# Moving one gate/up block between a down projection and its Wo part in a fused attention + GLU kernel

## The chip, the core and the metric

The program runs on one core of a Trainium2 chip. The metric is the device time of one execution in microseconds (us), lower is better. Engines are named as in the profile: PE (matrix engine, PEld its weight loads), DVE (vector), ACT (scalar, activations), POOL (GpSimd), SP (the queue that issues nearly all DMAs). All of them run their own instruction list strictly in the order in which the program was written; waiting is done with semaphores.

## The reference

One LayerNorm feeds two branches, and both are added to the input:

```
x  = A_x                              # 1 x 2048 x 640, bf16
xn = layernorm(x)                     # no weights, eps 1e-5
q, k, v = split(xn @ wqkv)            # 32 heads of 20
s  = q k^T * 20**-0.5, key j kept for query i if 0 <= i - j < 256
A  = (softmax(s) v) @ wo
B  = (sigmoid(xn @ w_gate) * (xn @ w_up)) @ w_down      # hidden width 1536
out = x + A + B
```

`B_x` is not used.

## The kernel before

**Tiling.** The 2048 rows are four chunks of 512. A chunk is four blocks of 128 rows (s = 0 to 3). Heads go in eight groups of four.

**Two streams of work.** The attention scores are the clock of the program. There are 76 scores steps, t = 0 to 75: chunk 0 has 0 to 15, chunk 1 has 16 to 35, chunk 2 has 36 to 55, chunk 3 has 56 to 75. A step is some 24 small matmuls (`ps`, L462), one big exponential on ACT (L467) and, for most steps, three masks on POOL (L470). The scores tile `ps` takes four PSUM banks and has one buffer, so the matmuls of step t+1 wait until the exponential of step t has read it. When all steps of two groups are through, `pv` (L487) multiplies with v (`acc`, L494), and DVE transposes the two sums (`t1`, L504).

Everything else is filler that PE does between two scores steps. It is written as generators that yield the PE time of each piece in ns: a projection `q` or `k` (5 matmuls, 1080), a `v` block (10 matmuls, 1360), gate `g` and up `u` of one of twelve gate/up blocks (1080 each; ACT makes the tanh `th`, DVE the product `h`; `th` has one buffer, L140), a quarter of a down projection `d` (6 matmuls, 816; four of them make the two column halves of one output block), and `W`, the ten matmuls with Wo that finish the output block (1360; then DVE adds x, L427, and SP stores, L436). The list of generators is at L642 to L662, and PE executes it in that order. At each step the loop at L678 gives out an allowance: the filler left up to the next output part (`out0`, `out1`, `out2`, or the end), divided by the steps left until it opens. Whole pieces are pulled until the allowance is used up (`credit`, L694); what is pulled too much is kept as debt. `out0` opens at step 17, `out1` at 36, `out2` at 56, each after the `pv` of the chunk's last two groups.

**Scaling the attention sums.** After `pv`, the division by the softmax sum (`scale_group`, L510: reciprocal, products into `on`, transposes into `oc`) isn't written at once. It is put into `fill.behind`, and each filler piece with a cost takes one entry off, after its own instructions (L542). The five tiles `oc` of a chunk are the weights of its `W` matmuls; the last one is complete only with the last group.

**LayerNorm.** Chunks 1 to 3 are normalised while the filler runs. `g_norms` (L333) has steps of no PE cost, called L (statistics on DVE), r (the inverse root on POOL), N (the normalised block on DVE) and T (`turn_block`, L275: a DMA transpose issued by SP into `xnT`). All four blocks of `xnT` must have landed before the first `q` of the chunk, since each matmul of a projection streams all 512 rows. `mix` (L564) puts one such step after every second piece of another generator. For chunk 2 (`norms2`) it starts in `gu1a` and goes on in `out0`.

**PSUM.** All other matmul results share a ring of four one-bank buffers (`ps_d`, L142): y0, y1 of an output block, pg, pu, pqk, pv, acc. A new tile takes the buffer of the fourth one before it and waits for its reader.

**The order that results** for the steps that the text speaks of. It is worked out from the costs and the allowance rule above; `S` is one scaled group, `P` the `pv` of two groups. A step's own scores come first, then the pieces:

```
 5: T N u S T T g S    13: v S v S          17: d S L r d S d
 6: u g u              14: v v              18: L r d W N d
 7: g u                15: g L u            19: d r N d d T N W
 8: q q P              16: g L r u P        20: d T N d d P
                                            21: T T d S W S d
36: d S d S T d d      56: d S d S d        22: d d d W
37: W T d d            57: d W              23: q q     (x of chunk 3 is loaded first)
```

In steps 12 to 14 this goes with `k k P`, `v v`, `v v`, where SP gets the loads of k and q of chunk 1 after the first and second `v`, and the load of Wo (four DMAs) at step 15. In step 62 there are two `d` alone.

Of the kernel before, what the change touches and what calls it, by code (L numbers as in the profile page):

```python
# [21 lines left out]
NG = H // HG  # L22
# [85 lines left out]
def kernel(  # L108
# [13 lines left out]
    out2 = out.flatten_outer_dims()  # L122
# [151 lines left out]
    def turn_block(c, s):  # L274
        nc.sync.dma_start(out=xnT[c][:, :, s * P:(s + 1) * P], in_=xns.pop((c, s)), transpose=True)  # L275
# [57 lines left out]
    def g_norms(c, turn):  # L333


        new_xnT(c)
        mv, rstd = {}, {}
        for k in range(SBC + 4):
            if k < SBC:
                mv[k] = ln_block(c, k)  # L340
            if 0 <= k - 1 < SBC:
                rstd[k - 1] = rstd_block(mv[k - 1])
            if k < SBC:
                yield 0
            if 0 <= k - 3 < SBC:
                norm_block(c, k - 3, mv[k - 3], rstd[k - 3])
                yield 0
            if turn and 0 <= k - 3 - 1 < SBC:
                turn_block(c, k - 3 - 1)

    def g_turns(c):
        for s in range(SBC):
            turn_block(c, s)
            yield 0

    def g_qk(c):
        for w in "qk":
            for m in range(DC):
                proj_block(w, c, m)
                if c == 0 and w == "q" and m == 1:  # L360
                    load_x(1)
                if w == "k" and m == 1:
                    spread("q", c, 0, GH if c else 2)
                yield 5 * MM
        if c == 0:
            spread("k", c, 0, 1)
            spread("k", c, 1, 3)
            spread("q", c, 2, 4)
            spread("k", c, 3, 4)
# [17 lines left out]
    def part(w, d, f):  # L387
        k, first = divmod(f * P, FS)
        return w[k][:, d, first:first + P]

    def g_gu(c, f0, f1):
        for f in range(f0, f1):
            pg = ps_d.tile([P, CW], FP32, name="pg", tag="d")
            for d in range(DC):
                nc.tensor.matmul(pg, lhsT=part(wg, d, f), rhs=xnT[c][:, d, :],  # L395
                                 start=(d == 0), stop=(d == DC - 1))
            th = tp.tile([P, CW], FP32, name="th")
            nc.scalar.activation(out=th, in_=pg, func=TANH, scale=0.5)  # L398
            yield 5 * MM
            pu = ps_d.tile([P, CW], FP32, name="pu", tag="d")  # L400
            for d in range(DC):
                nc.tensor.matmul(pu, lhsT=part(wu, d, f), rhs=xnT[c][:, d, :],  # L402
                                 start=(d == 0), stop=(d == DC - 1))
            h = hp.tile([P, CW], BF16, name="h")
            ht[c, f] = h
            nc.vector.scalar_tensor_tensor(out=h, in0=th, scalar=1.0, in1=pu, op0=ADD, op1=MULT)  # L406
            yield 5 * MM
# [6 lines left out]
    def down(c, s, y, cut):  # L414
        for f in range(FC):
            nc.tensor.matmul(y[:, 0:cut[1] - cut[0]], lhsT=ht[c, f][:, s * P:(s + 1) * P],  # L416
                             rhs=wd[:, f, cut[0]:cut[1]], start=(f == 0), stop=False)
            if f % 6 == 5:
                yield 6 * 136

    def add_wo(c, s, y, cut):
        for m in range(DC):
            nc.tensor.matmul(y[:, 0:cut[1] - cut[0]], lhsT=oc[c, m][:, s * P:(s + 1) * P],  # L423
                             rhs=wo[:, m, cut[0]:cut[1]], start=False, stop=(m == DC - 1))

    def add_x(c, s, y, cut, rows):
        nc.vector.scalar_tensor_tensor(  # L427
            out=rows[:, cut[0]:cut[1]], in0=y[:, 0:cut[1] - cut[0]], scalar=0.5,
            in1=xc[c][:, s, cut[0]:cut[1]], op0=MULT, op1=ADD)

    def new_rows():
        return lnp.tile([P, D], BF16, name="xn", bufs=5)

    def store(c, s, rows, cut=(0, D), queue=nc.sync):
        sb = c * SBC + s
        queue.dma_start(out=out2[sb * P:(sb + 1) * P, cut[0]:cut[1]], in_=rows[:, cut[0]:cut[1]])  # L436

    def outp(c, s, ys):
        rows = new_rows()
        for y, cut in zip(ys, HALVES):  # L440
            add_wo(c, s, y, cut)
        for y, cut in zip(ys, HALVES):
            add_x(c, s, y, cut, rows)
        store(c, s, rows)

    def g_out(c):
        for s in range(SBC):
            ys = [ps_d.tile([P, CW], FP32, name=f"y{i}", tag="d") for i in range(2)]
            for y, cut in zip(ys, HALVES):
                yield from down(c, s, y, cut)  # L450
            outp(c, s, ys)
            yield 10 * 136

# [33 lines left out]
    def pv(c, g, parts):  # L487
        acc = ps_d.tile([P, CW], FP32, name="acc", tag="d")
        flat = [(pt, *piece[1:]) for step, pt in parts for piece in step["pv"] if piece[0] == g]
        for k, (pt, r, q, n, col) in enumerate(flat):  # L490
            v = vt[c * SBC + r]
            for i in range(HG):
                h = g * HG + i
                nc.tensor.matmul(  # L494
                    acc[32 * i:32 * i + 32, q * U:(q + n) * U],
                    lhsT=v[:, h * VW:h * VW + 32], rhs=pt[:, i, col * U:(col + n) * U],
                    start=(k == 0), stop=(k == len(flat) - 1), skip_group_check=True)
        finish_group(c, g, acc)
# [3 lines left out]
    def finish_group(c, g, acc):  # L502
        t1 = np_.tile([P, 16, 32], FP32, name="t1")
        nc.vector.transpose(out=t1.rearrange("p b r -> p (b r)"), in_=acc)  # L504
        if c < NCH - 1 or g < NG - 2:
            fill.behind.append(lambda: scale_group(c, g, t1))
        else:
            scale_group(c, g, t1)
# [14 lines left out]
    class Fill:  # L523
        def __init__(self):
            self.parts = []
            self.behind = []
            self.done = set()
            self.shut = set()

# [8 lines left out]
        def one(self):  # L538
            label, gen, _ = self.parts[0]
            try:  # L540
                cost = next(gen)
                if cost and self.behind:  # L542
                    self.behind.pop(0)()
                self.parts[0][2] -= cost
                return cost
            except StopIteration:
                self.parts.pop(0)
                self.done.add(label)
                return 0
# [14 lines left out]
    def mix(a, b, first, every=1, rest=True):  # L564

        for k, cost in enumerate(a):
            yield cost
            if k >= first and (k - first) % every == 0:
                yield next(b, 0)
        if rest:  # L570
            yield from b
# [63 lines left out]
    fill = Fill()  # L635
    GU = 10 * MM
    OUT = 4 * 34 * 136
    def later(load, *args):
        load(*args)
        yield 0  # L640

    norms2 = g_norms(2, True)  # L642
# [5 lines left out]
    fill.add("qk1", g_qk(1), 50 * MM)  # L648
    fill.add("v1", g_v(1), 40 * 136)
    fill.add("wo", later(load_wo), 0)  # L650
    fill.add("gu1a", mix(g_gu(1, 0, 2), norms2, 0, 2, False), 2 * GU)
    fill.add("out0", mix(g_out(0), norms2, 0, 2), OUT)
    fill.add("x3", later(load_x, 3), 0)
    fill.add("qk2", g_qk(2), 50 * MM)
    fill.add("v2", g_v(2), 40 * 136)
    fill.add("gu1b", mix(g_gu(1, 2, 12), g_norms(3, False), 10), 10 * GU)
    fill.add("out1", mix(g_out(1), g_turns(3), 1, 3), OUT)
    fill.add("qk3", g_qk(3), 50 * MM)
    fill.add("v3", g_v(3), 40 * 136)
    fill.add("gu2", g_gu(2, 0, 12), 12 * GU)  # L660
    fill.add("out2", g_out(2), OUT)
    fill.add("gu3", g_gu(3, 0, 12), 12 * GU)  # L662

    todo = [(c, k, step) for c in range(NCH) for k, step in enumerate(steps_of(c))]
    ends = {}
# [13 lines left out]
    for t, (c, k, step) in enumerate(todo):  # L679
        if k == 0 and c > 0:  # L680
            fill.until(f"qk{c}")
        if k == 2 and c > 0:
            fill.until(f"v{c}")
        if t in due:
            fill.flush()
        for group in due.get(t, []):
            pv(*group, parts.pop(group))
            if group[1] == NG - 1:
                fill.shut.discard(f"out{group[0]}")
        made = (step, scores(c, step))  # L690
        for g in dict.fromkeys(piece[0] for piece in step["pv"]):
            parts.setdefault((c, g), []).append(made)
        last, label = next(x for x in cuts if t < x[0])
        credit += fill.left(label) / (last - t)  # L694
        credit = fill.pull(credit)
# [3 lines left out]
    c = NCH - 1  # L699
# [18 lines left out]
    s = SBC - 1  # L718
# [41 lines left out]
```

## Time and profile before

| what | value |
|---|---|
| runs | 317.76, 317.27, 316.70 us; median 317.27 us |
| the profiled execution's own time | 316.61 us |
| its span, first to last instruction | 314.9 us (1.7 us lie around it) |
| PE busy, as the profile counts | 305.2 us, 97% |
| DVE, ACT, POOL busy | 50%, 61%, 51% of the span |
| granted PE clock | 1.000 over the whole span |
| steps of chunk 0 and the filler before `out0` | 24.8 to 84.7 us |
| `out0` | 84.7 to 109.2 us |
| `out1` | 157.4 to 180.9 us |
| `out2` | 233.6 to 258.1 us |
| tail (last output blocks, no more scores) | from 292.2 us |

A line of the timeline gives start, duration, engine, source line, operation, output and inputs, and the count of instructions merged into it; in brackets stands the idle time of the engine before it and what ended it. Matmul records end at a modelled time: 128x320 matmuls start 0.136 us apart and 128x512 ones 0.216 us apart while a record lasts about 0.30 and 0.38 us. So the time that a stop really costs is read from start to start, and it is some 0.16 us more than the idle time in the brackets. A piece is followed by scores about 0.09 us later than the spacing alone would have it.

### The profile page before, as it was taken

To read this page: it belongs to the slowest core of one execution; us is meant where nothing else is said; L and a number is where in the kernel's file an instruction comes from. 1 tells how busy PE (TensorE), PEld (TensorE's weight loads), DVE (VectorE), ACT (ScalarE), POOL (GpSimd) and SP (SyncE) were. 2 spreads that over 40 slices of the span, in tenths; PEclk is the share of its full clock that TensorE was granted. 3 is DMA by queue.
4 is the path that set the end of the run, shared out by engine and by line. 5 is a ranking of instruction groups with operands and counts; after the bars stand their busy time and mean duration, and the time that the engine had idled before them with its cause. 6 is when DMAs were issued, how large, how long until landed. Compare 5 with 4: busy or idle time off the path is not lost.

```text
span 314.9 us, 10530 instructions
## 1 busy us (share of the span) xinstructions
PE 305.2 (97%) x4629; PEld 175.5 (56%) x4666; DVE 156.9 (50%) x313; ACT 192.2 (61%) x179; POOL 159.7 (51%) x257
## 2 busy tenths in 40 slices
PE   8999999999989999999999999999999999999996
PEld 3654444446557656554466756545466655454675
DVE  4531467547694545258571642627252614563054
ACT  5724776787743467757545457785766567979100
POOL 3000487586783653736856163652719473948000
PEclk9999999999999999999999999999999999999999
DMA  7985999525906454600016024510000010000002
GB/s 251 376 303 181 319 388 148 210 87 162 254 32 84 45 189 152 202 3 2 15 29 87 26 89 140 168 63 2 2 3 23 25 44 2 2 4 0 3 2 83
DMA packets 34669, 33.08 MB, mean 105 GB/s; under 512 B 10016, under 2 KB 34080, under 8 KB 34592
## 3 DMA queue, kind: packets, MB, share of 16 engines
q1 hardware_dynamic: 34192, 32.14, 35.9%
q8 instruction: 36, 0.59, 0.8%
q10 hardware_dynamic: 432, 0.28, 0.3%
q14 instruction: 9, 0.07, 0.1%
HBM read 21.00 MB, written 10.26 MB: 99 GB/s over the span
## 4 chain that ended last, share of the span: by engine, by line
PE 86%; DVE 5%; ACT 4%; POOL 2%; issue 2%; DMA 1%; ACTq 0%; DVEq 0%
PE pu L402 14%; PE pg L395 14%; PE pqk L291 14%; PE y L416 13%; PE ps L462 8%; PE pv L318 7%; PE acc L494 6%; PE y L423 6%; ACT pT L467 3%; PE d L416 2%; POOL pT L470 1%; DVE on L516 1%; DVE oc L520 1%; DMA xc<-in_A_x_dram 1%; DVE h L406 1%
## 5 line engine op out<-in xcount | busy, mean ns | idle before, releaser
L470 POOL TENSOR_SCALAR_AFFINE_SELECT pT<-pT 128x512 bf16<-128x512 bf16 (+2 forms) x192 | 145.3, 787 | 130.3 <-ACT pT L467 130.2
L467 ACT ACTIVATE pT<-ps 128x2048 bf16<-128x2048 f32 x76 | 142.7, 1877 | 65.8 <-PE ps L462 59.7
L406 DVE SCALAR_TENSOR_TENSOR h<-th,pu 128x512 bf16<-128x512 f32 x48 | 32.9, 686 | 63.9 <-ACT th L398 31.8
L402 PE MATMUL pu<-xnT,wu 128*128 128x512 bf16 x229 | 58.9, 380 | 0.7 <-issue 0.2
L395 PE MATMUL pg<-xnT,wg 128*128 128x512 bf16 x223 | 57.6, 380 | 1.6 <-issue 1.1
L416 PE MATMUL y<-wd,h 128*128 128x320 bf16 (+1 forms) x348 | 50.6, 297 | 0.5 <-issue 0.5
L291 PE MATMUL pqk<-xnT,wqkv 128*128 128x512 bf16 x191 | 45.4, 381 | 0.5
L416 PEld LDWEIGHTS <-h 128*128 128x128 bf16 x396 | 36.5, 98 | 15.0 <-issue 0.8
L398 ACT ACTIVATE th<-pg 128x512 f32<-128x512 f32 x48 | 28.6, 595 | 16.6 <-PE pg L395 10.7
L402 PEld LDWEIGHTS <-wu 128*128 128x128 bf16 x240 | 22.3, 98 | 26.4 <-issue 0.6
L395 PEld LDWEIGHTS <-wg 128*128 128x128 bf16 x240 | 21.6, 98 | 24.2 <-issue 0.2
L462 PEld LDWEIGHTS <-kT 20*64 20x64 bf16 x1856 | 20.9, 103 | 25.2 <-issue 23.4
L462 PE MATMUL ps<-qT,kT 20*64 20x128 bf16 (+4 forms) x1856 | 32.5, 239 | 1.1 <-ACT pT L467 1.1
L291 PEld LDWEIGHTS <-wqkv 128*128 128x128 bf16 x200 | 22.5, 119 | 18.2 <-issue 0.6
L504 DVE STREAM_TRANSPOSE t<-acc 128x512 f32<-128x512 f32 x32 | 21.7, 707 | 21.2 <-PE acc L494 21.1
L427 DVE SCALAR_TENSOR_TENSOR xn<-y,xc 128x320 bf16<-128x320 f32 (+1 forms) x29 | 13.7, 480 | 29.0 <-PE y L423 29.0
L516 DVE TENSOR_TENSOR on<-t,rec 128x320 bf16<-128x320 f32 (+4 forms) x48 | 26.1, 544 | 1.1
L318 PE MATMUL pv<-wqkv,xnT 128*128 128x320 bf16 x160 | 23.6, 300 | 0.0
L494 PE MATMUL acc<-pT,v 128*32 128x64 bf16 (+3 forms) x1376 | 23.2, 223 | 0.3
L494 PEld LDWEIGHTS <-v 128*32 128x32 bf16 x1376 | 18.6, 97 | 8.0 <-issue 2.6
L423 PE MATMUL y<-wo,oc 128*128 128x320 bf16 (+1 forms) x145 | 21.9, 297 | 0.9 <-DVE oc L520 0.9
L295 DVE CAST st<-pqk 128x512 bf16<-128x512 f32 x20 | 13.8, 690 | 12.0 <-PE pqk L291 12.0
(46 smaller groups left out, 150.5 us busy)
## 6 DMA issues: line engine op xcount, KB each, us to landing
qT<-sq SPq DMA_DIRECT2D x7, 512.0 KB, 5.4
sq<-st SPq DMA_DIRECT2D x20, 128.0 KB, 3.3
sk<-st SPq DMA_DIRECT2D x20, 128.0 KB, 3.3
out_dram<-xn SPq DMA_DIRECT2D x15, 160.0 KB, 1.8
kT<-sk SPq DMA_DIRECT2D x4, 512.0 KB, 6.7
wg<-in_B_w_gate_dram SPq DMA_DIRECT2D x2, 960.0 KB
wu<-in_B_w_up_dram SPq DMA_DIRECT2D x2, 960.0 KB, 9.3
xc<-in_A_x_dram SPq DMA_DIRECT2D x3, 640.0 KB, 5.5
```

The costliest lines, as they stand in the source:

```text
L291: nc.tensor.matmul(ps, lhsT=wt[:, m, :], rhs=xnT[c][:, d, :], start=(d == 0), stop=(d == DC - 1))
L318: nc.tensor.matmul(ps[:, 0:HALF], lhsT=xnT[c][:, d, s * P:(s + 1) * P], rhs=wqkv[:, d, 2 * D + hf * HALF:2 * D + (hf + 1) * HALF], start=( ...
L395: nc.tensor.matmul(pg, lhsT=part(wg, d, f), rhs=xnT[c][:, d, :], start=(d == 0), stop=(d == DC - 1))
L402: nc.tensor.matmul(pu, lhsT=part(wu, d, f), rhs=xnT[c][:, d, :], start=(d == 0), stop=(d == DC - 1))
L406: nc.vector.scalar_tensor_tensor(out=h, in0=th, scalar=1.0, in1=pu, op0=ADD, op1=MULT)
L416: nc.tensor.matmul(y[:, 0:cut[1] - cut[0]], lhsT=ht[c, f][:, s * P:(s + 1) * P], rhs=wd[:, f, cut[0]:cut[1]], start=(f == 0), stop=False)
L423: nc.tensor.matmul(y[:, 0:cut[1] - cut[0]], lhsT=oc[c, m][:, s * P:(s + 1) * P], rhs=wo[:, m, cut[0]:cut[1]], start=False, stop=(m == DC - 1))
L462: nc.tensor.matmul(ps[hf * U:(hf + 1) * U, i, col * U:(col + n) * U], lhsT=qk["k", kc, g // GH][32 * i:32 * i + DH, g % GH, key:key + U], ...
L467: nc.scalar.activation(out=pt[:, :, 0:CW], in_=ps, func=EXP, scale=SCALE)
L470: nc.gpsimd.affine_select(out=out, in_=in_, pattern=[[0, HG], [0, n], [sign, width]], compare_op=GE, fill=0.0, base=base, channel_multipli ...
L494: nc.tensor.matmul(acc[32 * i:32 * i + 32, q * U:(q + n) * U], lhsT=v[:, h * VW:h * VW + 32], rhs=pt[:, i, col * U:(col + n) * U], start=( ...
L516: nc.vector.tensor_tensor(out=on[m][:, :, slot:slot + n], in0=t1[:, :, first:first + n], in1=rec.to_broadcast([P, 16, n]), op=MULT)
```

## The change

Three edits, with no change in what is computed and none in the number of instructions on any engine:

1. `Fill.hurry`: after the `pv` of a chunk's last two groups, the first filler piece takes both scalings off the list, not one (and the flag falls with the next `pv`).
2. `g_out` takes a second generator, `between`, and runs it after the four `d` of block s = 0, ahead of its `W`. What runs there is one gate/up block: block 1 of chunk 1 in `out0` (it leaves `gu1a`, which stands before `out0`), block 0 of chunk 2 in `out1` and block 0 of chunk 3 in `out2` (these leave `gu2` and `gu3`, which stand behind).
3. `norms2` has one step left in `gu1a` (before: two) and starts in `out0` at its fifth piece instead of its first.

```diff
-    def g_out(c):
+    def g_out(c, between):
         for s in range(SBC):
             ys = [ps_d.tile([P, CW], FP32, name=f"y{i}", tag="d") for i in range(2)]
             for y, cut in zip(ys, HALVES):
                 yield from down(c, s, y, cut)
+            if s == 0:
+                yield from between
             outp(c, s, ys)
             yield 10 * 136
...
+            self.hurry = False
...
                 if cost and self.behind:
-                    self.behind.pop(0)()
+                    for _ in range(2 if self.hurry else 1):
+                        if self.behind:
+                            self.behind.pop(0)()
...
-    fill.add("gu1a", mix(g_gu(1, 0, 2), norms2, 0, 2, False), 2 * GU)
-    fill.add("out0", mix(g_out(0), norms2, 0, 2), OUT)
+    fill.add("gu1a", mix(g_gu(1, 0, 1), norms2, 0, 2, False), GU)
+    fill.add("out0", mix(g_out(0, g_gu(1, 1, 2)), norms2, 4, 2), OUT + GU)
...
-    fill.add("out1", mix(g_out(1), g_turns(3), 1, 3), OUT)
+    fill.add("out1", mix(g_out(1, g_gu(2, 0, 1)), g_turns(3), 1, 3), OUT + GU)
...
-    fill.add("gu2", g_gu(2, 0, 12), 12 * GU)
-    fill.add("out2", g_out(2), OUT)
-    fill.add("gu3", g_gu(3, 0, 12), 12 * GU)
+    fill.add("gu2", g_gu(2, 1, 12), 11 * GU)
+    fill.add("out2", g_out(2, g_gu(3, 0, 1)), OUT + GU)
+    fill.add("gu3", g_gu(3, 1, 12), 11 * GU)
...
         for group in due.get(t, []):
+            fill.hurry = group[1] == NG - 1
             pv(*group, parts.pop(group))
```

The costs given to the list change with it, so the allowance does too: before `out0` there are 37,840 ns of filler for 17 steps, where there were 40,000. By the same rule as above the order becomes:

```
 5: T N u S T T g S    13: k S v S          17: d S S d d
 6: u g                14: v                18: d g L r u
 7: u g                15: v v              19: W L r d d L r d
 8: u q P              16: g L u P          20: d N W d P
                                            21: r N d S d S T N d W
36: d S S d T d d      56: d S S d d        22: T N d d T T d
37: g T u W            57: d g              23: d W q   (x of chunk 3 is loaded before q)
38: d T d d            58: u W
```

Steps 0 to 5 are as before. The loads of k and q of chunk 1 now follow the `v` of steps 13 and 14, and the load of Wo comes at step 16. The two `d` alone are in step 63.

## The prediction

> **What bounds the kernel.** The first part of the page shows a PE that hardly stops, so only its waits can be won or lost:
>
> ```profile
> PE 305.2 (97%) x4629; PEld 175.5 (56%) x4666; DVE 156.9 (50%) x313; ACT 192.2 (61%) x179; POOL 159.7 (51%) x257
> ```
>
> Then I read PE's timeline around the output parts, where the change works (start, duration, operation, count, idle before):
>
> ```profile
> 87.95 0.45 PE L416 MATMUL y<-wd,h 128*128 128x320 bf16 x2
> 88.88 0.72 PE L416 MATMUL y<-wd,h 128*128 128x320 bf16 x4 [0.48 <-issue]
> 89.43 0.71 PE L423 MATMUL y<-wo,oc 128*128 128x320 bf16 x4
> 90.72 0.99 PE L423 MATMUL y<-wo,oc 128*128 128x320 bf16 x6 [0.58 <-DVE oc L520]
> ...
> 161.46 0.72 PE L423 MATMUL y<-wo,oc 128*128 128x320 bf16 x4
> 162.47 0.99 PE L423 MATMUL y<-wo,oc 128*128 128x320 bf16 x6 [0.29 <-DVE oc L520]
> ```
>
> The first W of `out0` and `out1` waits for its fifth `oc`; four matmuls go, then PE stands. Start to start: 90.72 - (89.43 + 4 x 0.136) = 0.75 us; 162.47 - (161.46 + 0.54) = 0.47. In `out0` there is a second stop, 88.88 - (87.95 + 2 x 0.136) = 0.66: the trace's semaphore records have the last of Wo's four loads landing at 88.84. `out2` has no such wait.
>
> Third, where PE waits for the exponential. In chunk 0, and in `out2`:
>
> ```profile
> 51.86 1.24 PE L402 MATMUL pu<-xnT,wu 128*128 128x512 bf16 x5
> 53.34 0.43 PE L462 MATMUL ps<-qT,kT 20*64 20x320 bf16 x24 [0.23 <-ACT pT L467]
> 54.79 1.24 PE L402 MATMUL pu<-xnT,wu 128*128 128x512 bf16 x5
> 56.54 0.42 PE L462 MATMUL ps<-qT,kT 20*64 20x320 bf16 x16 [0.51 <-ACT pT L467]
> ...
> 251.71 0.43 PE L462 MATMUL ps<-qT,kT 20*64 20x320 bf16 x24
> 254.26 0.43 PE L462 MATMUL ps<-qT,kT 20*64 20x320 bf16 x24 [0.39 <-ACT pT L467]
> ```
>
> 254.26 - 251.71 = 2.55 us is the shortest distance of two scores steps when ACT does nothing else: scores 0.36 leave 2.19, so a step with under 2.1 of filler stands still. 53.34 is later than PE's own work (51.86 + 1.08 + 0.09 = 53.03) by 0.31, 56.54 (54.79 + 1.17 = 55.96) by 0.58. ACT shows why:
>
> ```profile
> 50.92 0.60 ACT L398 ACTIVATE th<-pg 128x512 f32<-128x512 f32 x1 [1.72 <-DVE h L406]
> 51.41 1.87 ACT L467 ACTIVATE pT<-ps 128x2048 bf16<-128x2048 f32 x1
> ```
>
> `th` has one buffer; its tanh waited for `h`, which stood behind a normalisation on DVE, and the exponential of step 6 queued behind it, until 53.28.
>
> Last, SP and DVE in `out0`, and the first projection of chunk 2:
>
> ```profile
> 96.14 0.49 DVE L427 SCALAR_TENSOR_TENSOR xn<-y,xc 128x320 bf16<-128x320 f32 x1 [1.76 <-PE y L423]
> 96.83 0.49 DVE L427 SCALAR_TENSOR_TENSOR xn<-y,xc 128x320 bf16<-128x320 f32 x1 [0.19 <-PE y L423]
> ...
> 97.34 0.37 SPq L436 DMA_DIRECT2D out_dram<-xn  x1
> 97.77 5.13 SPq L275 DMA_TRANSPOSE xnT<-xn  x3
> ...
> 109.16 2.35 PE L291 MATMUL pqk<-xnT,wqkv 128*128 128x512 bf16 x9
> ```
>
> The last three transposes stand on SP behind a store that waits for DVE's addition. Their completions are recorded at 101.72, 102.99 and 105.73, so `q` at 109.16 found them 3.4 us old.
>
> **The change, part by part.** The work on every engine is the same, so the sum is one of PE's waits.
>
> *The W waits.* `oc` is complete 4.6 us after the pair's `pv` in `out1` (157.8 to 162.4). Behind `pv`, PE now has four d (3.26), the block (2.16) and three scores (1.08) ahead of W, 6.5 us with joints. Both scalings at once also take a statistics step of 1.1 us out from between them. Won: 0.75 + 0.47 = 1.22. The stop for Wo's load goes too if the load isn't later than PE: it is issued some 1 to 2 us later (below), W comes 6.7 us after scores 17 instead of 4.7. Won 0.66; if Wo is late, between 0 and 0.66. Together **-1.9**.
>
> *Chunk 0, steps 6 to 8.* The allowance falls by 2160/17 = 127 ns a step, and step 6 gives `u g` instead of `u g u`. Steps 0 to 5 are unchanged, so the exponential of step 6 ends at 53.28 as before, and scores 7 cannot start sooner than 53.34. PE is done at 51.95: the u that was there is now missing and is done later. **+1.1** (it is 1.08 exactly if ACT moves nothing; 0 as the other end).
>
> *Chunk 0, step 14.* One v alone: scores 0.36 + 1.36 + 0.09 = 1.81 us against 2.55. ACT has the two copies (0.58 and 0.43) between, but these end before its exponential must start. **+0.7** (0 to 1.0).
>
> So the block that left chunk 0, 2.16 us of PE, brings scores 17 forward from 84.7 only to some 84.3.
>
> *k of chunk 1.* Its last k block moves from step 12 to 13, its copy behind the exponential of step 13: stored near 75.1 instead of 71.9. The reload of k was issued 2.2 us after the landing of most of that store, at 76.42, and landed at 79.07, for scores at 80.95. Now I expect 79.9 to 82.1 for scores at 80.6: 0 to 1.6, I take **+0.2**, because the late half of the store before (one of 16 parts, at 76.34 instead of 74.8) needn't recur.
>
> *LayerNorm of chunk 2 later.* This is the large one. The transposes move from steps 19 to 21 to steps 21 and 22; q stays in step 23. The last three stand on SP behind the store of block 2, whose additions follow its W at the end of step 21. From that W's end to q, PE has only 0.09 + 0.36 + 2.45 + 0.09 + 0.36 + 0.82 + 1.36 = 5.5 us. The chain took 105.73 - 96.63 = 9.1 us from W's end in the trace (96.63 = start of W at 95.27 + 10 x 0.136); its first transpose issue lasted 2.49 us where the others took 1.2 to 1.3, so 7.9 without that. DVE is later now: behind `pv` it has the two t1 (done 0.84 after scores, as at 101.92), N 0.45, S 0.7, S 2.0 (104.23 to 106.24), N 0.45, so that the additions end some 0.45 late: 8.3. The first of them also frees the PSUM buffer that block 3 takes, about 0.3 us after PE wants it (**+0.3**, 0 to 0.5), which lengthens PE's way to 5.8. Then q waits 8.3 - 5.8 = 2.5. Ends: 2.0 (DVE not late) and 3.8 (a long first issue again); I take **+2.6**. POOL isn't it: the last r stands behind the masks of step 21 and is done before SP gets to it.
>
> In the trace a 160 KB store lands 1.8 us after its issue (median), a lone transpose of the same size after 2.6 (155.73 to 158.33), and one issued straight behind another after 4.1 (101.68 to 105.73). The Trainium skill (Advanced Engine Details and Errata, X-Bar Transpose (TRN2)) says instead that transposing DMAs are as fast as ordinary ones. By the rule the third would land 1.8 us after its issue, q would wait some 0.2 us, and the whole sum would be near +0.8; I go by the rows.
>
> *`out2`.* Step 57 becomes `d g`: 0.36 + 0.82 + 1.08 + 0.09 = 2.35 against 2.55. **+0.2** (0 to 0.3). The 0.48 at 254.26 (two d alone) only moves to step 63. In `out1`, W is followed by scores, so the PSUM buffer that the block took away costs nothing; its cover is that 0.36, without it under 0.1 (at 103.63 a d follows W with no stop, DVE being free). The transposes of chunk 3 keep two steps more than here.
>
> Sum: -1.9 + 1.1 + 0.7 + 0.2 + 2.6 + 0.3 + 0.2 = **+3.2 us**. On the profiled execution's 316.61 this is 319.8; that execution lies 0.66 under the median of the runs, so I forecast 317.27 + 3.2 = **320.5**.
>
> **Rivals.**
> (a) *The transposes are hidden after all*: they land within 5.8 us of W's end. For it: one alone needs only 2.6. Against: three in a row behind a store needed 7.9 or more. Then +0.6, 317.9, no change that can be told.
> (b) *Only the W waits count* (faster). Place: the first W of `out0` and `out1`; price -1.9, with 0.2 given back in `out2`, 315.6. It decides when all new waits together stay below 1.9, which needs q without a wait and at most half of chunk 0's. For it: the waits are real and their cover is ample. Against: scores 7 are tied to an exponential that nothing in steps 0 to 5 moves.
> (c) *The late loads add to it*: k of chunk 1 late by 1.6 and the long transpose issue, 3.8: 320.5 + 1.4 + 1.2 = 323.1. One part in 16 of both k stores did come late.
>
> **Chances and range.** Forecast 0.66, (a) 0.17, (b) 0.11, (c) 0.06. A measurement tells from no change what is over 0.3%, 0.95 us. Faster takes (b) and the edge of (a), 0.13; the same the rest of (a), 0.13; slower 0.74. The forecast's own range, from its terms' ends, is 319.0 to 322.0; for 8 in 10 it reaches over (a) and toward (c): 317.4 to 322.8.
>
> **What would show it.** Right: no idle time before the L423 matmuls of the first blocks; scores 7 still near 53.3 with over 1 us of idle; some 0.7 before scores 15; and 2 to 4 us of idle PE before the first L291 matmul of chunk 2, ended by the DMA into `xnT`, with three transposes issued on SP just behind a store. Wrong: if that idle time is under 1 us, the large term falls; if scores 7 come at 52, chunk 0's does.

## The result, and the profile after

| | time | ratio to the kernel before, 95% interval |
|---|---|---|
| kernel before | 317.28 us (median of 4) | |
| changed kernel | 317.57 us (median of 4) | 1.0009 [0.9991, 1.0027] |
| changed kernel, again on another occasion | 317.55 us (8) beside 316.67 us (25) | 1.0032 [1.0018, 1.0047] |

The change makes the kernel no faster: the two comparisons give 0.1% more, inside the noise, and 0.3% more. The forecast of +3.2 us was too high by more than 2 us. The profiled execution of the changed kernel took 317.62 us with a span of 315.9 us, against 316.61 and 314.9.

PE's timeline after, at the places that the prediction named (start, duration, operation, count, idle before):

```profile
51.04 1.24 PE L395 MATMUL pg<-xnT,wg 128*128 128x512 bf16 x5
53.61 0.43 PE L464 MATMUL ps<-qT,kT 20*64 20x320 bf16 x24 [1.33 <-ACT pT L469]
56.81 0.42 PE L464 MATMUL ps<-qT,kT 20*64 20x320 bf16 x16 [0.51 <-ACT pT L469]
...
75.50 1.53 PE L318 MATMUL pv<-wqkv,xnT 128*128 128x320 bf16 x10
77.65 0.43 PE L464 MATMUL ps<-qT,kT 20*64 20x320 bf16 x24 [0.62 <-ACT pT L469]
...
91.27 1.53 PE L423 MATMUL y<-wo,oc 128*128 128x320 bf16 x10
...
104.35 0.43 PE L464 MATMUL ps<-qT,kT 20*64 20x320 bf16 x24
104.71 2.62 PE L416 MATMUL y<-wd,h 128*128 128x320 bf16 x18
...
108.44 1.52 PE L423 MATMUL y<-wo,oc 128*128 128x320 bf16 x10
110.74 1.25 PE L291 MATMUL pqk<-xnT,wqkv 128*128 128x512 bf16 x4 [0.78 <-DMA xnT<-xn]
...
164.91 1.52 PE L423 MATMUL y<-wo,oc 128*128 128x320 bf16 x10
```

The two W waits are gone: the ten matmuls of W stand in one line, at 91.27 and 164.91, with nothing in brackets. Scores 7 and scores 15 wait for the exponential, and the first q of chunk 2 waits for the transposes. So the large terms of the prediction are all there (two small ones are not, see below), but the last one is far smaller than forecast: 110.74 - (108.44 + 10 x 0.136) = 0.94 us instead of 2.6. SP shows the order that was expected, a store and then three transposes, but these issue one behind the other with no long one among them:

```profile
104.98 0.34 SPq L436 DMA_DIRECT2D out_dram<-xn  x1
105.38 3.86 SPq L275 DMA_TRANSPOSE xnT<-xn  x3
```

Their completions are recorded at 108.00, 109.30 and 110.61.

Both traces can be compared piece by piece where the same work is behind PE. The lag of the changed kernel is 0.26 us at the first scores (the loads of the first rows; this part varies from run to run, up to 1.8 us in the traces below), 2.05 at scores 17 once the missing block is counted, 1.58 at q of chunk 2, 1.58 still at scores 30 and 35, 1.28 at scores 37, 0.80 to 0.82 in chunk 2's steps, and 1.00 from scores 65 to the end. Without the start that is +0.74. For the comparison of traces I use from here on the span less the start of the first scores: 283.48 us before, 284.22 changed, 284.17 changed again.

### The profile page after: what moved, and what is told of

It reads as the page before. It is cut to its first block, busy times and chain, and to the rows that moved or that the text cites. A ratio compares the mean times of both kernels' runs of the same rounds, so it can differ in the third digit from the quotient of the medians.

```text
span 315.9 us, 10526 instructions
## 1 busy us (share of the span) xinstructions
PE 304.8 (96%) x4627; PEld 175.8 (56%) x4666; DVE 156.1 (49%) x313; ACT 192.7 (61%) x179; POOL 160.1 (51%) x257
## 4 chain that ended last, share of the span: by engine, by line
PE 82%; ACT 6%; POOL 4%; DVE 3%; issue 2%; DMA 2%; SPq 1%; ACTq 0%; DVEq 0%
PE pu L402 15%; PE pg L395 14%; PE pqk L291 14%; PE y L416 11%; PE ps L464 7%; PE acc L496 6%; PE pv L318 6%; PE y L423 5%; ACT pT L469 5%; POOL pT L472 3%; PE d L416 2%; DMA xc<-in_A_x_dram 1%; DVE on L518 1%; DMA xnT<-xn 1%; SPq L275 1%
## 5 line engine op out<-in xcount | busy, mean ns | idle before, releaser
L518 DVE TENSOR_TENSOR on<-t,rec 128x320 bf16<-128x320 f32 (+4 forms) x48 | 24.8, 517 | 1.1
```

## The experiments

**The LayerNorm of chunk 2 early again (e1).**

```diff
-    fill.add("out0", mix(g_out(0, g_gu(1, 1, 2)), norms2, 4, 2), OUT + GU)
+    fill.add("out0", mix(g_out(0, g_gu(1, 1, 2)), norms2, 0, 2), OUT + GU)
```

> The changed kernel with one edit taken back: the LayerNorm steps of chunk 2 start at the first piece of out0 again, so all four transposes stand on SP before the store of block 2. Theory T (the changed kernel gave back 0.94 us at the first q of chunk 2, because the transposes land at 110.6 and PE is there at 109.8): that wait goes to 0, the statistics steps on DVE behind the two scalings bring no W wait back, and the time is 317.6 - 0.9 = 316.7. Rival C (the lost time is chunk 0's alone; q's wait only takes up slack that another engine would take up next): 317.6, with an equal wait elsewhere in steps 21 to 27.

Measured: 316.64 us beside 316.95, ratio 0.9976 [0.9949, 1.0002]; span from the first scores 283.23, 0.99 below the changed kernel. The waits of PE in this trace (line waited for, total, times, longest):

```profile
PE ps L464 <- ACT pT L469: 2.8, 4, 1.3
PE pwarm L235 <- DVE st L164: 1.3, 1, 1.3
PE pg L395 <- issue: 0.8, 5, 0.2
```

The wait for `xnT` is off the list, nothing has come in its place, and the statistics steps behind the scalings bring no W wait back. By the traces, edit 3 of the change was a loss of its own, of 0.94 us, and PE's wait there was real time.

**Both scalings at once, alone (e2).** The kernel before with edit 1 only.

```diff
                 if cost and self.behind:
-                    self.behind.pop(0)()
+                    for _ in range(2 if self.hurry else 1):
+                        if self.behind:
+                            self.behind.pop(0)()
...
         for group in due.get(t, []):
+            fill.hurry = group[1] == NG - 1
             pv(*group, parts.pop(group))
```

> The kernel before with only the first edit: both scalings behind the first piece. Theory W (the first W of out0 waits for oc because a statistics step of 1.1 us and the second reciprocal stand between the scalings): the 0.75 us wait in out0 goes, the 0.66 for Wo's load and the 0.47 in out1 stay; 317.3 - 0.75 = 316.5. Rival (the fifth oc isn't the last thing missing; Wo's load or DVE's additions take its place): 317.3, with the idle time moved by a few matmuls.

Measured: 316.95 beside 316.95 us, ratio 0.9994 [0.9962, 1.0025]. PE at the first W of `out0`:

```profile
88.10 0.45 PE L416 MATMUL y<-wd,h 128*128 128x320 bf16 x2
90.05 0.72 PE L416 MATMUL y<-wd,h 128*128 128x320 bf16 x4 [1.51 <-issue]
90.61 1.52 PE L423 MATMUL y<-wo,oc 128*128 128x320 bf16 x10
```

The wait for `oc` is gone, W runs through. But in this execution the last of Wo's four loads landed at 89.97 instead of 88.84, and PE stands 1.7 us for it (90.05 - 88.10 - 0.27), longer than both stops of the kernel before together (1.40). This was the rival's outcome. The first W of `out0` waits for whichever comes later, `oc` or Wo, and Wo's landing varies: 87.2 to 92.3 in the eleven traces in which its load wasn't taken forward. Part of what edit 1 wins in one run is taken by Wo in the next. At the first W of `out1` the stop for `oc` is as before (at 162.88, 0.29 in brackets). So edit 1 alone removes the wait for `oc` in `out0`, and in `out1` it takes the block.

**Two buffers for th (e3).** The changed kernel, with

```diff
-    op = pool("op", 7)
+    op = pool("op", 6)
...
-    tp = pool("tp", 1)
+    tp = pool("tp", 2)
```

> The changed kernel with two buffers for th (and six instead of seven for oc, to make room, which nothing waits for). Theory A (scores 7 and 8 wait because the tanh of one block stands on ACT, waiting for h of the block before, ahead of the exponential): scores 7 follow scores 6 by some 2.6 us instead of 4.0 and scores 8 lose their 0.6 too, so 1.4 + 0.6 = 2.0 us less; 317.6 - 2.0 = 315.6. The 0.7 before scores 15 stays. Rival (DVE's or POOL's backlog behind pv holds the next exponential in any case, through the masks or h): 317.3 to 317.6, with the idle time at the same two places or one step later.

Measured: 316.42 beside 316.95 us, ratio 0.9967 [0.9943, 0.9990]; span from the first scores 283.52, only 0.7 below the changed kernel. PE's timeline from step 6 on:

```profile
50.71 0.42 PE L464 MATMUL ps<-qT,kT 20*64 20x320 bf16 x16
51.07 1.25 PE L402 MATMUL pu<-xnT,wu 128*128 128x512 bf16 x5
52.16 1.24 PE L395 MATMUL pg<-xnT,wg 128*128 128x512 bf16 x5
53.33 0.43 PE L464 MATMUL ps<-qT,kT 20*64 20x320 bf16 x24
```

Scores 7 follow scores 6 by 2.62 us instead of 4.02, and scores 8 lose their wait as well: theory A holds for its mechanism, 1.4 + 0.6 = 2.0 us. The rest of the gain is missing because scores 6 themselves came 1.2 us late. The waits of the same trace say why, the second half of the up weights landed late in it (42.05; between 39.7 and 41.2 in the traces that don't wait for it):

```profile
PE pu L402 <- DMA wu<-in_B_w_up_dram: 1.1, 1, 1.1
```

That load is issued near 30 us, before anything that the edit changes; it was late in one other run with two `th` (e10) and on time in two (e7, e8), and PE waits for it in e9 too, which has one `th`. So it is a matter of the run.

**The LayerNorm later still (e4).**

```diff
-    fill.add("out0", mix(g_out(0, g_gu(1, 1, 2)), norms2, 4, 2), OUT + GU)
+    fill.add("out0", mix(g_out(0, g_gu(1, 1, 2)), norms2, 6, 2), OUT + GU)
```

> The changed kernel with the LayerNorm of chunk 2 two pieces later still (start at the seventh piece of out0): now all four transposes stand behind the store of block 2. Theory T (a transpose lands 2.6 us after its issue and issues are 1.3 us apart, without a queue in between): the fourth lands 1.3 us later, q waits 0.9 + 1.3 = 2.2 us, 318.9. Rival Q (transposes queue up behind one another, 2.7 us for each further one, as the last one in the trace of the kernel before): 0.9 + 2.7 = 3.6, 320.3. Rival C (the wait is slack that something else uses): 317.6.

Measured: 320.74 beside 316.95 us, ratio 1.0099 [1.0063, 1.0135]. In the trace the wait is

```profile
PE pqk L291 <- DMA xnT<-xn: 2.2, 1, 2.2
```

in the idle column, 2.36 from start to start, against 2.24 by theory T and 3.6 by Q. The four transposes landed 2.59 to 2.66 after their issues, in steps of 1.3. So in this trace they don't queue behind each other. Another 0.7 us is lost at 90.34, in the block ahead of the first W; the profile calls that stop "issue", and what ended it isn't seen. The profiled execution took 319.42, the six timed ones 320.5 to 321.3. The granted clock was 1.000 in the former and 0.995 in each of the latter, so the ratio isn't the price of the wait alone. The timed ones have no trace; e9 below shows what such a figure can stand for.

**The changed kernel again (e5).** No edit.

> The changed kernel itself once more, beside the kernel before on the same chip, for a narrower interval and as the base of the next three. Theory (PE's waits as the two profiles show them: +1.1 at scores 7, +0.7 at scores 15, +0.9 at q of chunk 2, +0.2 in out2, against -1.4 and -0.5 at the first W of out0 and out1, in sum +1.0, less where Wo's load lands later than at 88.8 in the kernel before, since only that kernel waits for it): 0 to 1.0 us above the kernel before, with the same places of idle time. Rival (something not seen in the profile): outside of that, or waits at other places.

Measured: 317.55 beside 316.67 us, ratio 1.0032 [1.0018, 1.0047]: +0.9 us, inside the theory's range, and the waits of PE are the known ones, apart from the start:

```profile
PE ps L464 <- ACT pT L469: 2.8, 4, 1.3
PE pwarm L235 <- DVE st L164: 1.3, 1, 1.3
PE pv L318 <- ACT xnT L272: 1.2, 1, 1.2
PE pqk L291 <- DMA xnT<-xn: 0.8, 1, 0.8
PE pt L271 <- DVE xn L263: 0.6, 1, 0.6
```

The third and the last line belong to the first 11 us, where the first scores came 1.5 us later than in the other execution.

**The block back in front of out0 (e6).** The changed kernel, with

```diff
-    fill.add("gu1a", mix(g_gu(1, 0, 1), norms2, 0, 2, False), GU)
-    fill.add("out0", mix(g_out(0, g_gu(1, 1, 2)), norms2, 4, 2), OUT + GU)
+    fill.add("gu1a", mix(g_gu(1, 0, 2), norms2, 0, 2, False), 2 * GU)
+    fill.add("out0", mix(g_out(0, ()), norms2, 0, 2), OUT)
```

> The changed kernel with block 1 of chunk 1 back in front of out0 (nothing between there, LayerNorm steps from the first piece on); both scalings at once and the blocks of out1 and out2 stay. Theory A (the block's 2.16 us were covering waits for the exponential in steps 6 and 14): against the changed kernel -1.8 in chunk 0, -0.9 at q of chunk 2, and back comes only the wait for Wo's load at the first W, 0.7 to 1.7 as in the run with the first edit alone: 1.0 to 2.0 below the changed kernel, some 0.3 to 1.0 below the kernel before. Rival (chunk 0 is bound by PE after all): no gain in chunk 0, 0.2 below to 0.8 above the changed kernel.

Measured: 315.94 beside 316.67 us, ratio 0.9978 [0.9963, 0.9994]; span from the first scores 282.40, 1.8 below the changed kernel. The waits of PE:

```profile
PE pwarm L235 <- DVE st L164: 1.3, 1, 1.3
PE ps L464 <- ACT pT L469: 1.1, 3, 0.5
PE y L416 <- issue: 0.5, 1, 0.5
```

Chunk 0's waits fall from the changed kernel's 2.8 (with `out2`'s 0.4 in both) to 1.1; the third line is Wo's load, landing at 89.1 here, 0.6 from start to start. Against e1, which differs by the place of this block alone, it is 0.84 us less: a gain of 1.78 in chunk 0, of which 0.62 is lost at Wo and 0.31 at the `pv` of step 35 (below). So, with one `th`, the block was worth more to PE in chunk 0 than between the down projection and W.

**Early LayerNorm and two th (e7); the kernel before with two th (e8).** The edits of e1 and e3 together; and that of e3 on the kernel before.

> The changed kernel with the LayerNorm of chunk 2 early again and two buffers for th: the waits at scores 7 and 8 (1.4 + 0.6) and at q (0.9) should both be gone, leaving 0.7 at scores 15, 0.2 and 0.5 in out2. Theory: 317.5 - 2.9 = 314.6, 2 us or more below the kernel before. Rival (weights come late once PE is faster: the second half of the up weights in chunk 0, Wo at the first W): part of it goes there, 315.5 to 316, with idle time ended by a DMA.

> The kernel before with two buffers for th. Theory A: its own waits at scores 7 and 8 (0.3 + 0.6) go, 317.0 - 0.9 = 316.1, unless Wo's load, which then meets PE earlier, takes back up to that much at the first W of out0. If the run beats e7, the change is of no use even with its two waits mended; the theory has it 1.0 to 1.5 above e7. Rival (th isn't what holds the exponential): no difference to the kernel before, idle time at scores 7 and 8 as it was.

Measured: e7 315.27 us, ratio 0.9948 [0.9934, 0.9963]; e8 316.26 us, ratio 0.9985 [0.9968, 1.0002], both beside 316.67. From the first scores 281.68 and 282.37, 1.8 and 1.1 below the kernel before. e7 missed its 314.6 by 0.7: 0.2 to 0.3 of it is Wo's load at the first W (landed at 90.12, PE there), the start was 1.1 later in its trace. PE's waits behind the start, in e7, then in e8:

```profile
PE ps L464 <- ACT pT L469: 1.0, 2, 0.6
```

```profile
PE y L423 <- DVE oc L520: 1.0, 1, 1.0
PE ps L462 <- ACT pT L467: 0.4, 1, 0.4
```

In both, scores 7 and 8 wait no more. In e8 Wo landed at 87.2, and the whole loss at the first W is `oc` again, 1.2 us from start to start. With the wait in chunk 0 mended by other means, the change as a whole (with the early LayerNorm) does pay: e7 is 1.0 us below e8 by the timed runs and 0.7 by the traces, where 1.0 to 1.5 was expected. That it is the block in `out0` that pays isn't shown. Edit 1 alone took the wait for `oc` away in e2, the block of `out1` covers the stop there, and the 0.7 us before scores 15, which block 1 of chunk 1 covered in front of `out0`, are still lost in e7. No run has two `th` and edit 1 without any block.

**The instruction fetch moved (e9).** This one is about why the transposes were faster than forecast. In the trace of the kernel before, the second and fourth transpose of chunk 2 took 3.95 and 4.05 us to land, in the changed kernel none of the last three over 2.65. The DMA view tells a difference: in the stretch of the three transposes before (97 to 106 us), and after (105 to 111 us):

```profile
q1 hardware_dynamic: 2304, 0.82, 79.2%
q8 instruction: 2, 0.03, 2.2%
...
xnT<-xn SPq DMA_TRANSPOSE x3
```

```profile
q1 hardware_dynamic: 2160, 0.66, 49.3%
...
xnT<-xn SPq DMA_TRANSPOSE x3, 2.6
```

Before, two packets of the queue that brings instructions ran in that stretch, at 98.09 (1.74 us long) and 102.61 (1.48 us). After there was none between 102.0 and 114.5. To move them, the changed kernel got 72 tiny matmuls at its start, which compute nothing that is used:

```diff
+    for _ in range(3):
+        ps = ps_d.tile([P, CW], FP32, name="pwarm", tag="d")
+        for k in range(24):
+            nc.tensor.matmul(ps[:, 0:64], lhsT=warm[:, 0:P], rhs=warm[:, 0:64], start=(k == 0), stop=(k == 23))
```

> The changed kernel with 72 tiny warm-up matmuls (144 PE instructions) more at its very start; they compute nothing that is used and lengthen the start by some us, so only the wait of chunk 2's first q is read. Theory F (a transpose takes 2.6 us from issue to landing, and some 4 when PE's instruction fetch on the queue q8 runs beside it; the kernel before had two such fetches beside its last three transposes, the changed kernel none between 102.0 and 114.5): the fetch that came at PE instruction 2733 falls 144 earlier in the program, on the second or third transpose; one of the three takes 4 us instead of 2.6 and q waits 2.2 to 2.6 us instead of 0.94. Rival (the long transposes of the kernel before come from the order of its stores, not from the fetch): all three at 2.6, q waits 0.9 as before.

Measured in its trace, DMA view from 105 to 114 us, and PE:

```profile
q8 instruction: 1, 0.02, 0.9%
...
xnT<-xn SPq DMA_TRANSPOSE x3, 3.9
```

```profile
110.33 1.52 PE L428 MATMUL y<-wo,oc 128*128 128x320 bf16 x10
113.70 1.25 PE L296 MATMUL pqk<-xnT,wqkv 128*128 128x512 bf16 x5 [1.86 <-DMA xnT<-xn]
```

The fetch is at 109.75 now, between the issues of the second and the third transpose. They took 2.61, 4.21 and 3.68 us, and q waits 113.70 - (110.33 + 1.36) = 2.0 us instead of 0.94. Theory F stands, a little under its 2.2 to 2.6. (The fetch didn't move by just the 144 instructions; where exactly it comes was predicted poorly.) The execution took 322.29 us, with its longer start, and its trace shows one more price of a long wait. Behind q's first five matmuls and one scores step the granted clock of PE is 0.50 for 3.4 us. PE's timeline there, and that stretch (of the figures in the second line, PE busy is the second and the granted clock the third from the end):

```profile
115.24 4.04 PE L296 MATMUL pqk<-xnT,wqkv 128*128 128x512 bf16 x10
115.30:118.70 3.40, 3.40 (x12) 1.21 (x10) 1.07 (x2) 1.88 (x1) 1.25 (x3) 0.50 0.44 161
```

The same ten matmuls take 2.35 us in e4 (from 114.09). So the stretch costs 1.7 us, and by that one alone the mean clock of a span of 318 us would be 0.995, the figure of e4's timed executions. That those had such a stretch behind q is an estimate from this, not seen; e4's traced execution, with a wait of 2.36 us, had none.

**A version from all of this (e10).** e6 with two `th` and six `oc`, no block in `out2`, and the load of Wo taken forward:

```diff
-    fill.add("out2", g_out(2, g_gu(3, 0, 1)), OUT + GU)
-    fill.add("gu3", g_gu(3, 1, 12), 11 * GU)
+    fill.add("out2", g_out(2, ()), OUT)
+    fill.add("gu3", g_gu(3, 0, 12), 12 * GU)
...
-    fill.add("wo", later(load_wo), 0)
...
                 proj_block(w, c, m)
+                if c == 1 and w == "q" and m == 3:
+                    load_wo()
```

> A version from what the runs showed: the first edit (both scalings at once) and the block of out1 stay; block 1 of chunk 1 is back in front of out0 with the LayerNorm early, out2 has no block (it had no wait there to cover), th has two buffers, and Wo is loaded from the middle of chunk 1's q projection, 12 us earlier. Theory: from the run with the block back, 315.9, less 0.9 (scores 7 and 8), 0.6 (Wo's load) and 0.2 (out2): 314.2, below all others. Rival (the early load of Wo delays q or k of chunk 1, which the scores of step 16 need): 315 or more, with idle time before scores 16 ended by a DMA.

Measured: 315.39 beside 316.89 us, ratio 0.9937 [0.9910, 0.9965]. It beats both kernels, by 0.6% the one before, but not its own forecast, and it is no better than e7. Its PE waits:

```profile
PE pu L404 <- DVE mv L249: 1.4, 1, 1.4
PE pwarm L235 <- DVE st L164: 1.3, 1, 1.3
PE ps L466 <- ACT pT L471: 0.4, 1, 0.4
```

Neither the rival's wait nor Wo's is there. The first line is put down to DVE, but DVE's statistics have nothing to do with that matmul; its up weights are recorded as landed at 42.29, and the matmul starts at 42.34. It is the late load of e3 once more. The lowest timed run, 314.16, may be what is left without it; it has no trace. Less this stop (1.46 us from start to start) the trace of e10 would be 0.9 us below that of e7, one more sign that with two `th`, too, the block is no better placed in `out0`; but e10 differs from e7 in the load of Wo and in `out2` as well.

## Why the prediction was wrong

Where PE lost or won time, by the prediction's terms and by the two traces, start to start:

| term | forecast | traces |
|---|---|---|
| first W of `out0` (`oc` 0.75, Wo 0.66) | -1.4 | -1.40 |
| first W of `out1` | -0.5 | -0.46 |
| scores 7 (1.40 for 0.31) | +1.1 | +1.09 |
| scores 15 | +0.7 | +0.70 |
| k of chunk 1 | +0.2 | 0 |
| PSUM buffer of block 3 | +0.3 | 0 |
| first q of chunk 2 | +2.6 | **+0.94** |
| step 57 of `out2` | +0.2 | +0.18 |
| `pv` of step 35 | not seen | -0.31 |
| sum | +3.2 | +0.74 |

**Right.** The order of the pieces, worked out from the allowance, and with it the places of the four waits that came or grew (scores 7, scores 15, q, step 57); the other two that were forecast, k and the PSUM buffer, didn't come. The W waits went. In `out1` it is the block that covers the wait, as given; in `out0` edit 1 alone is enough for `oc` (e2), and the block covers Wo's landing. Chunk 0 lost what was forecast, and e3, e7 and e8 show that the cause is the single `th`, e6 that the block's place decides it. The changed kernel started scores 17 at 84.57, of which 0.26 is the start: 84.3, as forecast. The late LayerNorm does make q wait, e1 takes the wait away and e4 more than doubles it.

**The step that failed** is the size of q's wait: "Ends: 2.0 (DVE not late) and 3.8 (a long first issue again); I take +2.6". It measured 0.94, under the 1 us below which the prediction itself gave the term up. It was made from one chain in one trace, 9.1 us from the end of W to the last landing, less 1.24 for one long issue, plus 0.45 for DVE. The chain took 110.61 - 104.26 = 6.35 us. Of the difference of 1.95 to the 8.3 that I used, 1.4 was a second delay in the chain of the kernel before: its last transpose took 4.05 us, as the second fetch ran beside it. I had seen the lone 2.6 and the 4.05 side by side and read the latter as the price of queueing, which e4 refutes and e9 replaces by the fetch. Another 0.45 is DVE: the two scalings of step 21 took 2.3 us instead of 2.7, and the additions, from 104.07 on, ended 2.05 us after the start of W, as in the trace before. For the same reason the PSUM buffer was free (104.71 follows 104.35 by the usual 0.36), so PE's way was 5.5 and not 5.8. Some 0.1 of the chain's difference is left over. The low end, 2.0, was wrong as well: it kept the fetch's delay as if it were part of every such chain.

With 0.9 for q and nothing for the buffer the sum would have been near +1.2. Rival (a), which had the transposes hidden, came nearer in time than the forecast but isn't what happened. The prediction's other reckoning, a transpose landing in 1.8 us and a sum near +0.8, also comes near the measured time, but by chance: q waited 0.94 us and not 0.2, and no transpose of chunk 2 or 3 in any trace landed in under 2.57 us.

**The smaller ones.** k of chunk 1 landed at 79.98, for scores at 80.83; the late part didn't come again in the last store of k (all 16 completions lie between 77.10 and 77.28, its reload was issued at 77.35), and a margin of 0.85 was left. The 0.31 at step 35 is won, not lost: before, the 96 matmuls of that `pv` took 1.82 us, after 1.52. In every trace with the block in front of `out0` (e2, e6, e8, e10) they are slow. The trace of the kernel before shows where: half-way the matmuls pause for 0.33 us, until 156.59. The second `acc` takes the PSUM buffer of a `pu`, and DVE's `h`, which reads it, ends at 156.55; it stood behind a normalisation that had waited 2.45 us for POOL (`rstd`). POOL works on no mask from 154.6 to 159.9. No run moved that `h`, so this cause is read, not tried.

**Trace and timing.** The traces give +0.74 without the start, the timed runs +0.3 and +0.9 us. A likely reason for the spread, not tested: the first W of the kernel before pays for a late Wo load (e2), the changed kernel only beyond about 1 us of it, and both pay for the loads of the first 40 us.

## What to carry to other kernels

Work put between a producer and its consumer is taken from somewhere; ask what it hid there. Here the block covered a wait of 1.08 us for the exponential in chunk 0 and another of 0.7, and it cost about as much to take it away as the W waits were worth; with the coupling removed (a second buffer for a tile of 2 KB per partition) the kernel with the moved blocks and the early LayerNorm beats the kernel before by 1.4 us, though which of its edits earns that was not separated. When a chain of transfers is priced from one trace, look at each link in every place where it occurs, and at the other queues beside it, before a long one is taken as its price. And a stop on PE can cost more than its length: behind the 2.0 us of e9 the granted clock was halved for 3.4 us.

## What the runs showed of the hardware

A DMA transpose of 128 x 640 bf16 took either 2.6 us from issue to landing or 3.1 to 4.5, and which of the two goes with the instruction fetch. In the twelve traces of this study there are 96 transposes of chunks 2 and 3. 49 had no packet of the instruction queues beside them in their first 2.35 us, and they took 2.57 to 2.69 us. 47 had one; 43 of these took 3.06 to 4.52, and the four where the packet came only 2.3 us after the issue or later took 2.61 to 2.72 (the limit of 2.35 us was read off these same traces; that moving the fetch moves the delay is shown by e9 alone). In 42 of the 43 delayed ones all 16 completions came within 0.3 us of one another, so the whole transfer was late. Stores of the same size landed after 1.8 us in the median; of 179, 27 took 2.0 to 3.8 us, 26 of these had such a packet beside them, and in each of the 26 just one of the 16 completions was late. The packets are about 16 KB each (36 of them, 0.59 MB, in the page of either kernel), and they moved when instructions were added to PE alone (e9).

A wait on a DMA can show up on PE some matmuls too early. In the kernel before, e2 and e6 the stop for Wo stands in the middle of the six `d` matmuls ahead of W (x2, then x4), is called "issue", and ends when Wo lands, though these six don't read Wo.
